# Thresholded attention and SwiGLU on one core: alternating two column tiles of TensorE, and a GpSimd comparison with one operation instead of two

## The chip, the cores and the metric

The kernel runs on one core of a Trainium2 chip. The metric is the device time of one execution in microseconds (us). Lower is better. The program is one launch; matmuls run on TensorE (PE), whose weight loads are shown apart (PEld); VectorE (DVE), ScalarE (ACT) and GpSimd (POOL) do the rest, and SyncE (SP) issues most DMAs.

## The reference

Eight batches, eight heads, 576 rows of queries, keys and values with 64 elements each; then a feed-forward layer over the 4608 rows of 512.

```python
scores = (1 / sqrt(64)) * q @ k.T                      # per batch and head, 576 x 576
thresh = max(scores, axis=-1) - tau                    # tau = 0.02
scores = where(scores >= thresh, scores, -1e9)
attn   = exp(scores - max(scores))
attn   = attn / (sum(attn) + 1e-9)
x      = attn @ v                                      # heads side by side: 4608 x 512
xn     = x / sqrt(mean(x * x) + 1e-6) * rms_g
out    = (silu(xn @ w_gate) * (xn @ w_val)) @ w_out    # 512 -> 1536 -> 512, float32
```

## The kernel before

**Chunks and steps.** The 576 rows of a batch are 4 chunks of 128 rows ("m", ordinary) and 64 last rows. The last rows of two batches together make one "virtual" chunk ("v"): partitions 0 to 63 belong to the first batch, 64 to 127 to the second. There are 32 ordinary and 4 virtual chunks. A step is one chunk with one of 4 pairs of heads, so there are 144 steps; 16 of them are virtual.

**One step.** `emit_s` (line 569) makes the scores of two heads in two PSUM tiles `s_ps`. `emit_softmax` (from line 586) goes on: VectorE reads the scores, negates and scales them into `ssb` and gives each row's minimum `mx` (line 592); GpSimd adds tau to it, `nth` (line 599). Then a head goes one of two ways. In way "p" ScalarE alone drives the elements past the threshold down (line 610) and takes the exponential (lines 614 and 617). In way "g" ScalarE takes the exponential into `esb` (line 629), while GpSimd compares the scores with the threshold, which gives a mask of ones and zeros in `wsb` (line 643), and then multiplies mask by exponential (line 648). From step 16 on the second head of every other step goes way "g", 64 masks in all; the rest goes way "p". The weights `wsb` are turned by a DMA transpose on SP's queue (line 677; in early steps by TensorE, line 662) into `wt`.

**Weights times values.** `emit_av` runs for two steps at a time, so there are 72 blocks, 8 of them virtual. For each step and head, five matmuls accumulate over the 576 keys: four with 65 columns (64 values and a column of ones that gives the sum; line 700) for each head, and one with 130 columns for the last 64 keys of both heads (line 696). In an ordinary block a step has 9 matmuls with weights of 128 columns. In a virtual block the two batches have different values, so the weights are taken 64 columns at a time: rows 0 to 63 of the result with the values of the one batch, rows 64 to 127 with those of the other. These are two column tiles of TensorE, each with 9 matmuls a step, 36 a block.

**Feed-forward.** Groups of 2 or 4 chunks go through `emit_ffn`: gate (line 795), values (line 800), gating on ScalarE and VectorE (lines 809, 812, 817), output (line 865, in the last group line 840).

**Order.** Nothing is ordered by dependence alone. Every operation is entered with an engine, a cost in ns from the table `COST`, a priority and its dependences. `order_ops` (line 44) then plays the whole program through with these costs and gives each engine a fixed order, and hands out the four PSUM buffers `ring` and the places in queues. So a changed cost moves operations on every engine. The cost of a virtual block is twice `av_virt`, that of a mask `mask_g`, 1740 ns. On the chip the engines wait for each other by semaphores, in that order.

Of the kernel before, what the change touches and what calls it, by code (L numbers as in the profile page):

```python
# [11 lines left out]
ALU = mybir.AluOpType  # L12
# [1 line left out]
SEM = 160.0  # L14
SLACK = 0.0
COST = dict(
    s_main=932.0, s_virt=900.0, tr_qk=530.0, tr4=230.0, tr_full=440.0, av_main=310.0, av_virt=480.0, ffn4=216.0, warm=3500.0,
    ttr=690.0, evac_qk=600.0, evac_half=380.0, evac_kt=350.0, prelu=700.0, exp2=1250.0, exp1=690.0, exp0=690.0,
    mask_d=750.0, mask_g=1740.0, take_g=1300.0, trw=510.0, evac_w=450.0, evac_wp=900.0, rz=180.0, xmul=420.0, sq=800.0, xn=720.0,
    pool_tiny=270.0, pool_mean=800.0, pool_dma=850.0, cast_v=650.0, cast_vt=420.0, cast_w=720.0,  # L20
# [107 lines left out]
def kernel(  # L128
# [13 lines left out]
    B, H, S, D = q.shape  # L142
# [40 lines left out]
    ssb = [sb(f"ssb{i}", [128, 2, S]) for i in range(NSS)]  # L183
    NES = 3
    mx = [sb(f"mx{i}", [128, 2]) for i in range(6)]
    nth = [sb(f"nth{i}", [128, 2]) for i in range(6)]
    esb = [sb(f"esb{i}", [128, S], FP16) for i in range(NES)]
    NW = 3
# [39 lines left out]
    for i in range(B // 2):  # L228
        chunks += [("m", 2 * i, c) for c in range(4)]
        at = V_AFTER[i]  # L230
# [355 lines left out]
    def emit_softmax(s, so):  # L586

        a = s % NSS
        m = s % 6
        for h in range(2):  # L590
            def ttr(o, h=h):
                nc.vector.tensor_tensor_reduce(  # L592
                    out=ssb[a][:, h], in0=s_ps[h][:, ROW_AT:ROW_AT + S], in1=zrow, scale=-1.0 / 8.0, scalar=3.0e38,
                    op0=ALU.add, op1=ALU.min, accum_out=mx[m][:, h:h + 1])

            ttr_of[s, h] = add("DVE", COST["ttr"], s - 1, [so, o_c] + exp_of.get(s - NSS, []), ttr)

        def nthr(o):
            nc.gpsimd.tensor_scalar(out=nth[m], in0=mx[m], scalar1=tau, scalar2=None, op0=ALU.add)  # L599

        tn = add("POOL", COST["pool_tiny"], s - 4, [ttr_of[s, 0], ttr_of[s, 1]], nthr)
        wfree = [w_read.get(s - NW)]
        done = []
        ways = WAYS[s % len(WAYS)] if s >= FIRST else "pp"
        pls = []
        for h in range(2):
            way = ways[h]
            if way == "p":
                def prelu(o, h=h):
                    nc.scalar.activation(out=ssb[a][:, h], in_=ssb[a][:, h], func=PRELU, scale=-1.0,  # L610
                                         bias=nth[m][:, h:h + 1], **PRELU_KW)

                def ex(o, h=h):
                    nc.scalar.activation(out=wsb[s % NW][:, h], in_=ssb[a][:, h], func=AF.Exp)  # L614

                def ex2(o):
                    nc.scalar.activation(out=wsb[s % NW], in_=ssb[a], func=AF.Exp)  # L617

                pls.append(add("ACT", COST["prelu"], s + 0.5, [tn], prelu))
                if ways != "pp":  # L620
                    done.append(add("ACT", COST["exp0"], s + 0.5, pls + wfree, ex))
                elif h:
                    done.append(add("ACT", COST["exp2"], s + 0.5, pls + wfree, ex2))
            else:
                es = pre.get("n", 0) % NES
                pre["n"] = pre.get("n", 0) + 1

                def ex(o, h=h, es=es):
                    nc.scalar.activation(out=esb[es], in_=ssb[a][:, h], func=AF.Exp, scale=-1.0,  # L629
                                         bias=nth[m][:, h:h + 1])  # L630

                e = add("ACT", COST["exp1"], s + 0.4, [tn, pre.get(("es", es))], ex)
                if way == "d":
                    def mask(o, h=h, es=es):
                        nc.vector.scalar_tensor_tensor(
                            out=wsb[s % NW][:, h], in0=ssb[a][:, h], scalar=nth[m][:, h:h + 1], in1=esb[es],
                            op0=ALU.is_le, op1=ALU.mult)

                    st = add("DVE", COST["mask_d"], s + 0.4, [e] + wfree, mask)
                    done.append(st)  # L640
                else:
                    def mask(o, h=h):
                        nc.gpsimd.tensor_scalar(  # L643
                            out=wsb[s % NW][:, h], in0=ssb[a][:, h], scalar1=nth[m][:, h:h + 1], scalar2=1.0,
                            op0=ALU.is_le, op1=ALU.mult)

                    def take(o, h=h, es=es):
                        nc.gpsimd.tensor_tensor(out=wsb[s % NW][:, h], in0=wsb[s % NW][:, h], in1=esb[es],  # L648
                                                op=ALU.mult)

                    mk = add("POOL", COST["mask_g"], s + 0.4, [tn] + wfree, mask)
                    st = add("POOL", COST["take_g"], s + 0.4, [e, mk], take)
                    done.append(mk)
                pre["es", es] = st
                done.append(st)
        exp_of[s] = done

        if s < N_PE or s < N_ALT and s % 2:
            def tr(o):
                for j in range(9):  # L660
                    r, c = divmod(j, 5)
                    nc.tensor.transpose(ring[o.slot[r]].bitcast(FP16)[:, 128 * c:128 * c + 128],  # L662
                                        wsb[s % NW].rearrange("p h s -> p (h s)")[:, 128 * j:128 * j + 128], id16)

            t = add("PE", COST["trw"], s + 2.4, done + av_of.get(s - NWT, []), tr, ring="R", nring=2)
            w_read[s] = t
            w_ready[s] = []
            for r, (lo, hi) in enumerate(((0, 5), (5, 9))):
                def ev(o, r=r, lo=lo, hi=hi):
                    eng = nc.gpsimd if W_EVAC[r] == "POOL" else nc.vector  # L670
                    eng.tensor_copy(out=wt[s % NWT][:, lo:hi], in_=ring[t.slot[r]].bitcast(FP16)[
                        :, 0:128 * (hi - lo)].rearrange("p (c n) -> p c n", n=128))

                w_ready[s].append(add(W_EVAC[r], COST["evac_w" if W_EVAC[r] == "DVE" else "evac_wp"], s + 2.4, [t], ev, frees=(t, r)))
        else:
            def tdma(o):
                nc.sync.dma_start_transpose(out=wt[s % NWT], in_=wsb[s % NW].rearrange("p h s -> p (h s)"))

            t = add("SP", COST["sp_tr"], s, done + av_of.get(s - NWT, []), tdma, dma=DMA_NS['wt'])
            w_read[s] = t  # L680
            w_ready[s] = [t]

    def emit_av(s):

        ci, p1 = steps[s]
        kind, b, c = chunks[ci]
        hp = p1 // 2

        def fn(o):
            for i in range(2):  # L690
                w, p = wt[(s - 1 + i) % NWT], p1 - 1 + i
                rows = [(slice(0, 128), b % 2)] if kind == "m" else [(HALF[e], e) for e in range(2)]
                for rs, vi in rows:

                    at = 2 * i * (D + 1)
                    nc.tensor.matmul(ring[o.slot[0]][rs, at:at + 2 * (D + 1)], w[:, 4, rs],  # L696
                                     va[vi][:, p, 8:10].rearrange("p e d -> p (e d)"), start=True, stop=False)
                    for h in range(2):
                        for j in range(4):
                            nc.tensor.matmul(ring[o.slot[0]][rs, at:at + D + 1], w[:, 5 * h + j, rs],  # L700
                                             va[vi][:, p, 2 * j + h], start=False, stop=(h == 1 and j == 3))
                        at += D + 1

        bs = [b] if kind == "m" else [2 * b, 2 * b + 1]
        deps = w_ready[s - 1] + w_ready[s] + [x for bb in bs for i in range(2) for x in v_ready[bb, p1 - i]]
        o = add("PE", 2 * COST["av_main" if kind == "m" else "av_virt"], s + AV_PRIO, deps, fn, ring="R",
                mode=0 if kind == "m" else 3)
        for i in range(2):
            av_of[s - i] = [o]
            for bb in bs:  # L710
                last_av[bb, p1 - i] = last_av.get((bb, p1 - i), []) + [o]

        r = rz[len(half_ev) % 3]

        def half(_):
            o3 = ring[o.slot[0]][:, 0:4 * (D + 1)].rearrange("p (h d) -> p h d", d=D + 1)
            nc.vector.reciprocal(out=r, in_=o3[:, :, D])
            nc.vector.tensor_tensor(  # L718
                out=xsb[ci % 2][:, 256 * hp:256 * hp + 256].rearrange("p (h d) -> p h d", d=D),
                in0=o3[:, :, 0:D], in1=r[:, :, None].to_broadcast([128, 4, D]), op=ALU.mult)  # L720

        half_ev.append(add("DVE", COST["rz"] + COST["xmul"], s + HALF_PRIO, [o] + x_done.get(ci - 2, []), half,
                           frees=(o, 0)))
# [179 lines left out]
    groups, at = [], 0  # L903
# [157 lines left out]
```

## Time and profile before

| | |
|---|---|
| median of 3 runs | 568.4 us (568.31 to 568.87) |
| the profiled execution's own time | 568.4 us |
| its span, first to last instruction | 566.3 us |
| TensorE clock granted | 1.00 |
| busy: PE, PEld | 557.7 us (98%), 318.3 us (56%) |
| busy: DVE, ACT, POOL | 425.1 us (75%), 458.1 us (81%), 354.1 us (63%) |
| masks, line 643 | 64, mean 2219 ns |
| line 700, tiles of 64 columns | 256 matmuls; of 128 columns 1024 |

The times of instructions come from the one profiled execution, so they are set against its 568.4 us; 2.1 us of that lie outside the span. Matmuls are pipelined: an instruction's time in the profile is from its start to its modelled end, and the next one usually starts long before that. What a block of matmuls costs is therefore read from its start to the start of the next. In a row such as `128*64 128x65`, the first pair is the rows and columns of the tile of TensorE, the second the partitions and elements that stream through it.

### The profile page before, as it was taken

How to read it: one execution, taken by the hardware profiler on the slowest of the kernel's cores; microseconds unless marked ns; L12 is line 12 of the kernel's file. 1: busy time of each engine (PE TensorE's matmuls, PEld its weight loads, DVE VectorE, ACT ScalarE, POOL GpSimd, SP SyncE). 2: the span in 40 equal slices, each digit the busy share in tenths (PEclk: the TensorE clock that was granted, in tenths of full speed). 3: DMA queues.
4: the chain of work that ended last, by engine and by line, in shares of the span. 5: the costliest groups of instructions: out<-in, count | busy, mean ns of one | idle time of the engine just before them, and what ended most of it. 6: DMA issues, size and time to landing. Idle time of an engine off the chain costs nothing.

```text
span 566.3 us, 15217 instructions
## 1 busy us (share of the span) xinstructions
PE 557.7 (98%) x5768; PEld 318.3 (56%) x5768; DVE 425.1 (75%) x1091; ACT 458.1 (81%) x741; POOL 354.1 (63%) x462
## 2 busy tenths in 40 slices
PE   8999999999999999999999999999999999999997
PEld 4756666757666555545555455545555444444674
DVE  4989977859968588658985789668966886587354
ACT  5999989897989787888888898798988888785332
POOL 2378956996777467766677676766776765662000
PEclk9999999999999999999999999999999999999999
DMA  9999999779987598879977699888998444552201
GB/s 195 268 298 251 154 205 203 142 155 180 209 181 114 113 174 150 165 161 191 164 153 192 113 165 172 186 178 144 182 183 194 95 94 112 150 86 61 85 38 38
DMA packets 270025, 89.08 MB, mean 157 GB/s; under 512 B 252544, under 2 KB 262272, under 8 KB 269952
## 3 DMA queue, kind: packets, MB, share of 16 engines
q1 hardware_dynamic: 267168, 86.02, 74.3%
q0 software_dynamic: 1600, 1.57, 1.8%
q8 instruction: 45, 0.74, 0.6%
q10 hardware_dynamic: 1184, 0.52, 0.3%
q14 instruction: 28, 0.23, 0.2%
HBM read 37.75 MB, written 9.44 MB: 83 GB/s over the span
## 4 chain that ended last, share of the span: by engine, by line
PE 91%; DVE 3%; ACT 2%; issue 2%; DMA 1%; POOL 1%; SPq 0%; DVEq 0%; ACTq 0%; POOLq 0%
PE s_ps L569 28%; PE ring L795 16%; PE ring L800 16%; PE ring L865 15%; PE ring L700 6%; PE ring L304 2%; PE ring L696 2%; DVE ssb L592 1%; DMA stage<-in_moe_w_gate_dram 1%; PE s_ps L800 1%; PE s_ps L840 1%; PE s_ps L865 1%; PE ring L662 1%; PE ring L365 1%; ACT ssb L610 1%
## 5 line engine op out<-in xcount | busy, mean ns | idle before, releaser
L592 DVE CUSTOM_DVE_ANT_0 ssb<-s_ps,zrow 128x576 f32<-128x576 f32 x288 | 207.0, 752 | 62.5 <-PE s_ps L569 52.1
L610 ACT ACTIVATE ssb<-ssb,nth 128x576 f32<-128x576 f32 x224 | 166.2, 767 | 41.6 <-POOL nth L599 41.2
L569 PE MATMUL s_ps<-qkt 64*64 64x288 f32 (+1 forms) x1792 | 168.9, 417 | 1.6 <-DVE mx L592 1.5
L643 POOL TENSOR_SCALAR wsb<-ssb,nth 128x576 f16<-128x576 f32 x64 | 142.0, 2219 | 8.4 <-DMA wt<-wsb 3.0
L569 PEld LDWEIGHTS s_ps<-qkt 64*64 64x64 f32 (+1 forms) x1792 | 80.0, 140 | 63.8 <-DVE mx L592 16.5
L795 PE MATMUL ring<-xnT,wg 128*128 128x256 f16 (+1 forms) x564 | 114.4, 325 | 0.3 <-DVE xsb L718 0.3
L800 PE MATMUL ring<-xnT,wv 128*128 128x512 f16 (+1 forms) x528 | 110.4, 332 | 0.0
L812 DVE SCALAR_TENSOR_TENSOR sl<-th,ring 128x256 f32<-128x256 f32 (+1 forms) x141 | 77.0, 546 | 37.0 <-ACT th L809 36.3
L599 POOL TENSOR_SCALAR nth<-mx 128x2 f32<-128x2 f32 x144 | 31.9, 221 | 107.6 <-DVE mx L592 86.8
L617 ACT ACTIVATE wsb<-ssb 128x1152 f16<-128x1152 f32 x80 | 93.0, 1162 | 3.2 <-DMA wt<-wsb 1.1
L865 PE MATMUL ring<-wo,hf 128*128 128x512 f16 x384 | 90.0, 380 | 0.0
L648 POOL TENSOR_TENSOR wsb<-wsb,esb 128x576 f16<-128x576 f16 x64 | 81.8, 1278 | 9.7 <-ACT esb L629 5.2
L809 ACT ACTIVATE th<-ring 128x256 f32<-128x256 f32 (+1 forms) x141 | 67.2, 478 | 24.8 <-PE ring L795 20.1
L817 DVE TENSOR_TENSOR hf<-ring,sl 128x512 f16<-128x512 f32 (+1 forms) x132 | 74.9, 567 | 9.3 <-PE ring L800 0.5
L800 PEld LDWEIGHTS <-wv 128*128 128x128 f16 x576 | 52.2, 98 | 44.5 <-issue 14.0
L795 PEld LDWEIGHTS <-wg 128*128 128x128 f16 x576 | 51.9, 98 | 42.3 <-issue 12.3
L865 PEld LDWEIGHTS <-hf 128*128 128x128 f16 x408 | 37.3, 98 | 47.0 <-issue 7.0
L629 ACT ACTIVATE esb<-ssb,nth 128x576 f16<-128x576 f32 x64 | 49.2, 768 | 6.0 <-POOL nth L599 5.7
L700 PE MATMUL ring<-va,wt 128*128 128x65 f16 (+1 forms) x1264 | 52.8, 193 | 0.0
L700 PEld LDWEIGHTS <-wt 128*128 128x128 f16 (+1 forms) x1280 | 48.7, 100 | 4.3 <-issue 1.2
L614 ACT ACTIVATE wsb<-ssb 128x576 f16<-128x576 f32 x64 | 43.6, 681 | 1.6
L696 PE MATMUL ring<-va,wt 128*128 128x130 f16 (+1 forms) x158 | 35.1, 227 | 1.1 <-ACT qTv L473 1.1
(68 smaller groups left out, 446.2 us busy)
## 6 DMA issues: line engine op xcount, KB each, us to landing
vst<-in_v_dram SPq DMA_DIRECT2D x32, 256.0 KB, 3.5
qkn<-in_k_dram SPq DMA_DIRECT2D x31, 256.0 KB, 4.2
out_dram<-osb SPq DMA_DIRECT2D x31, 256.0 KB, 2.7
qkn<-in_q_dram SPq DMA_DIRECT2D x28, 256.0 KB, 4.1
stage<-in_moe_w_gate_dram SPq DMA_DIRECT2D x6, 512.0 KB, 5.9
stage<-in_moe_w_val_dram SPq DMA_DIRECT2D x6, 512.0 KB, 6.0
wt<-wsb SPq DMA_TRANSPOSE x128, 3.1
wo<-in_moe_w_out_dram POOLq DMA_DIRECT2D x4, 384.0 KB, 6.7
```

The source lines that it names most:

```text
L569: nc.tensor.matmul(s_ps[h][rows, ROW_AT + n * part:ROW_AT + n * part + n], lhs(hs), kT[i][p][h][hs, n * part:n * part + n], start=True, st ...
L592: nc.vector.tensor_tensor_reduce(out=ssb[a][:, h], in0=s_ps[h][:, ROW_AT:ROW_AT + S], in1=zrow, scale=-1.0 / 8.0, scalar=3.0e38, op0=ALU.a ...
L610: nc.scalar.activation(out=ssb[a][:, h], in_=ssb[a][:, h], func=PRELU, scale=-1.0, bias=nth[m][:, h:h + 1], **PRELU_KW)
L617: nc.scalar.activation(out=wsb[s % NW], in_=ssb[a], func=AF.Exp)
L643: nc.gpsimd.tensor_scalar(out=wsb[s % NW][:, h], in0=ssb[a][:, h], scalar1=nth[m][:, h:h + 1], scalar2=1.0, op0=ALU.is_le, op1=ALU.mult)
L648: nc.gpsimd.tensor_tensor(out=wsb[s % NW][:, h], in0=wsb[s % NW][:, h], in1=esb[es], op=ALU.mult)
L700: nc.tensor.matmul(ring[o.slot[0]][rs, at:at + D + 1], w[:, 5 * h + j, rs], va[vi][:, p, 2 * j + h], start=False, stop=(h == 1 and j == 3))
L795: nc.tensor.matmul(ring[o.slot[0]][:, 0:n], wg[d][:, fs], xnT[slot][:, d, 0:n], start=(d == 0), stop=(d == 3))
L800: nc.tensor.matmul(ring[o.slot[0]][:, 0:n], wv[d][:, fs], xnT[slot][:, d, 0:n], start=(d == 0), stop=(d == 3))
L812: nc.vector.scalar_tensor_tensor(out=sl[i][:, 0:n], in0=th[i][:, 0:n], scalar=1.0, in1=ring[g.slot[0]][:, 0:n], op0=ALU.add, op1=ALU.mult)
L817: nc.vector.tensor_tensor(out=hf[hi][:, 0:n], in0=ring[vv.slot[0]][:, 0:n], in1=sl[i][:, 0:n], op=ALU.mult)
L865: nc.tensor.matmul(ring[(first or o).slot[0]], hf[hs[fc][0]][:, 128 * j:128 * (j + 1)], wo[:, fc], start=(fc == 0), stop=(fc == NFC - 1))
```

## The change

Two edits, and one entry of the planner's table that goes with the first.

In a virtual block the loop over the two column tiles is moved inside: the two matmuls with 130 columns come first, one for each tile, and then for each head and each quarter of the keys a matmul for the first tile and one for the second. The matmuls are the same, 36 a block, and each tile's own order is kept. In an ordinary block there is one tile, and its order is unchanged. The table's `av_virt` goes from 480 to 320 ns, by which the planner makes another order for all engines from the first virtual block on.

GpSimd's comparison of scores with the threshold loses its second operation, a multiplication by 1.0. The result is the same mask. Its entry in the table, 1740 ns, stays.

```diff
-    ... av_main=310.0, av_virt=480.0, ffn4=216.0, ...
+    ... av_main=310.0, av_virt=320.0, ffn4=216.0, ...

                     def mask(o, h=h):
                         nc.gpsimd.tensor_scalar(
-                            out=wsb[s % NW][:, h], in0=ssb[a][:, h], scalar1=nth[m][:, h:h + 1], scalar2=1.0,
-                            op0=ALU.is_le, op1=ALU.mult)
+                            out=wsb[s % NW][:, h], in0=ssb[a][:, h], scalar1=nth[m][:, h:h + 1], scalar2=None,
+                            op0=ALU.is_le)

                 rows = [(slice(0, 128), b % 2)] if kind == "m" else [(HALF[e], e) for e in range(2)]
+                at = 2 * i * (D + 1)
                 for rs, vi in rows:
-
-                    at = 2 * i * (D + 1)
                     nc.tensor.matmul(ring[o.slot[0]][rs, at:at + 2 * (D + 1)], w[:, 4, rs],
                                      va[vi][:, p, 8:10].rearrange("p e d -> p (e d)"), start=True, stop=False)
-                    for h in range(2):
-                        for j in range(4):
+                for h in range(2):
+                    for j in range(4):
+                        for rs, vi in rows:
                             nc.tensor.matmul(ring[o.slot[0]][rs, at:at + D + 1], w[:, 5 * h + j, rs],
                                              va[vi][:, p, 2 * j + h], start=False, stop=(h == 1 and j == 3))
-                        at += D + 1
+                    at += D + 1
```

More of the change, by code (lines that the diff above doesn't have):

```diff
@@ L16 @@
 COST = dict(
-    s_main=932.0, s_virt=900.0, tr_qk=530.0, tr4=230.0, tr_full=440.0, av_main=310.0, av_virt=480.0, ffn4=216.0, warm=3500.0,
+    s_main=932.0, s_virt=900.0, tr_qk=530.0, tr4=230.0, tr_full=440.0, av_main=310.0, av_virt=320.0, ffn4=216.0, warm=3500.0,
     ttr=690.0, evac_qk=600.0, evac_half=380.0, evac_kt=350.0, prelu=700.0, exp2=1250.0, exp1=690.0, exp0=690.0,
```

## The prediction

> **What bounds the kernel now.** I read the page's busy table and chain first, then the stretches by time, then the blocks that the change touches, one by one.
>
> ```profile
> span 566.3 us, 15217 instructions
> PE 557.7 (98%) x5768; PEld 318.3 (56%) x5768; DVE 425.1 (75%) x1091; ACT 458.1 (81%) x741; POOL 354.1 (63%) x462
> PE 91%; DVE 3%; ACT 2%; issue 2%; DMA 1%; POOL 1%; SPq 0%; DVEq 0%; ACTq 0%; POOLq 0%
> ```
>
> TensorE is busy for 98% and is 91% of the chain that ended last. Its time is the kernel's time, and other engines count only where they make it wait. The stretches say where that is (columns: length; busy time and count of PE, PEld, DVE, ACT, POOL; clock; DMA).
>
> ```profile
> 150.00:200.00 50.00, 48.94 (x543) 31.05 (x543) 36.18 (x101) 42.92 (x73) 33.52 (x40) 1.00 0.77 147
> 200.00:300.00 100.00, 100.00 (x994) 52.95 (x992) 79.94 (x191) 84.51 (x132) 68.34 (x86) 1.00 0.85 166
> ```
>
> From 200 us on TensorE never pauses. Busy time hides short pauses, since the modelled end of a matmul runs on after it, so I also compared every block of matmuls, start to next start, with the fastest of its kind: 10.2 us are lost before 60 us, 7.9 between 60 and 200, 3.7 after that. GpSimd masks exist only from 60.0 to 507.6 us (line 643).
>
> **The weights times values of the virtual chunks.** There are 4 such chunks, of 4 head pairs; a block does two pairs, so there are 8 blocks of 36 matmuls. The chain shows one, and what follows it:
>
> ```profile
> 99.11 0.17 PE ring L696
> ...
> 99.90 0.27 PE ring L700 x10
> 100.17 0.38 PE s_ps L569
> ```
>
> From 99.11 to 100.17 the chain is in this block alone: 1.06 us. Start to next start the 8 blocks take 1.063 to 1.069 us, 8.5 us together. How much of that is one tile waiting for the other? The timeline of TensorE shows the four turns of this block, then one of its weight loads (PEld), and last a block of an ordinary chunk (128 columns, half the matmuls):
>
> ```profile
> 99.04 0.24 PE L696 MATMUL ring<-va,wt 128*64 128x130 f16 x1
> 99.12 0.32 PE L700 MATMUL ring<-va,wt 128*64 128x65 f16 x5
> 99.25 0.24 PE L696 MATMUL ring<-va,wt 128*64 128x130 f16 x1
> 99.47 0.24 PE L696 MATMUL ring<-va,wt 128*64 128x130 f16 x1
> 99.68 0.24 PE L696 MATMUL ring<-va,wt 128*64 128x130 f16 x1
> ...
> 99.25 0.11 PEld L696 LDWEIGHTS <-wt 128*64 128x64 f16 x1
> ...
> 95.33 0.23 PE L696 MATMUL ring<-va,wt 128*128 128x130 f16 x1
> 95.64 0.22 PE L696 MATMUL ring<-va,wt 128*128 128x130 f16 x1
> 96.03 0.45 PE L569 MATMUL s_ps<-qkt 64*64 64x288 f32 x1
> ```
>
> In the ordinary block nine matmuls take 0.31 us (95.33 to 95.64). In the virtual block a new turn of nine, of the same 650 moving columns, starts every 0.21 us. So a column tile already starts while the other still has three or so matmuls left: the two tiles do run side by side, but for only a third of the time, as far as the queue looks ahead. The last turn, with nothing behind it, takes 0.42 us to the next operation (99.68 to 100.10), of which some 0.1 us is the change of tile shape and stays.
>
> Matmul by matmul the partner is always next in the queue, and each tile has its 18 matmuls to itself. A tile then needs what an ordinary block needs, 0.70 us (95.33 to 96.03), plus about 0.03 for a first load that is not hidden: 0.73. Saving 1.066 - 0.73 = 0.33 us a block, **2.6 us** for eight. Bounds: at best 0.70 a block, 2.9 us saved; at worst the tiles take strict turns and lose the overlap that they have: four times 0.31 and 0.1 for the change of shape, 1.34 us a block, 2.2 us lost. I take 2.6, since the loads are seen overlapping: the load of line 696 for the second tile starts at 99.25, inside the first tile's row of matmuls (99.12 to 99.44), and those keep their pace. The score blocks also alternate over four 64x64 tiles and take 1.13 us for 16 matmuls, ones that stream over the same rows among them.
>
> A rule speaks against this. The Trainium skill, "TensorE: Matmul & The Clock Gate", Part 3 (The mechanism), says that weight loads overlap running matmuls only where the row group differs; both tiles here use all 128 rows. By that rule the tiles would take strict turns, and this term would be the loss of 2.2 us. The row at 99.25 is against it, so the measurement decides.
>
> **GpSimd's comparison with one operation.** The mask loses its second operation, a multiplication by 1.0. The rows of GpSimd that bear on it:
>
> ```profile
> L643 POOL TENSOR_SCALAR wsb<-ssb,nth 128x576 f16<-128x576 f32 x64 | 142.0, 2219 | 8.4 <-DMA wt<-wsb 3.0
> L487 POOL TENSOR_SCALAR va<-vst 128x512 f16<-128x512 f32 x32 | 20.0, 625 | 12.6 <-DMA vst<-in_v_dram 11.0 <-DMA vtl<-in_v_dram 0.5
> L487 POOL TENSOR_SCALAR va<-vtl 64x256 f16<-64x256 f32 x16 | 6.5, 404 | 1.1 <-DMA vtl<-in_v_dram 0.5
> ```
>
> Two multiplications cost (625 - 404) / 256 = 0.86 ns an element over some 183 ns fixed; compare and multiply cost (2219 - 183) / 576 = 3.5. Dropping one multiplication at half of 0.86 saves 0.25 us; at half of 3.5 it saves 1.0. The planner's table holds 1740 ns for this mask, and its other GpSimd costs stand 16 to 27 ns above what they measure (cast_w 720 to 693, take_g 1300 to 1278, cast_v 650 to 625), so 1740 reads like a one-operation mask of about 1.72 us, 0.5 less. I take that. No one-operation form of this size is in the trace (the only one, line 599, has 2 elements and 221 ns), so it can also be slower: bounds 1.2 to 3.0 us, the upper end being the same step the other way by 0.8.
>
> 64 masks by 0.5 is 32 us of GpSimd, but GpSimd is 1% of the chain. It counts where the threshold nth (line 599) is queued behind a mask or its product on GpSimd, and ScalarE, and then TensorE, wait for that nth. GpSimd's timeline shows it at one of TensorE's pauses:
>
> ```profile
> 169.97 1.28 POOL L648 TENSOR_TENSOR wsb<-wsb,esb 128x576 f16<-128x576 f16 x1
> 171.33 0.22 POOL L599 TENSOR_SCALAR nth<-mx 128x2 f32<-128x2 f32 x1
> ```
>
> The chain has the scores' minimum ready at 170.08, but nth runs only at 171.33, once the product of line 648 is through; at 173.8 TensorE loses 1.2 us. Between 60 and 200 us nine pauses are over 0.3 us. If all nine shrank by 0.5 that would be 4.5 us; if none, nothing. In some of them nth stands behind other work, or a DVE or DMA comes last, so I take about a quarter to a third, **1.3 us**.
>
> **The order.** av_virt goes from 480 to 320 in the planner, used twice for a block, so every engine's order after the first virtual block (about 99 us) is new. The work is not: the same matmuls, with 97 score blocks on four tiles instead of 96 (1.13 against 1.07 us each: 0.06 us). With each kind at its duration, TensorE's listed work falls by 2.6 us, all of it the virtual blocks. Score blocks move ahead of feed-forward work by up to 6 us in the middle. On SP a load of k now waits behind one more transpose of weights, on GpSimd two casts of v stand ahead of a mask instead of after it. Their cover is the TensorE work that lies between a score block and the weights times values that need it: 10.9 to 18.3 us in the old order from step 16 on, 11.2 to 18.3 in the new; the path of mask, product and transpose (2.2, 1.3 and 3.1 us) is 6.6 us. I take 0, with 2 us to either side.
>
> **The sum.** The profiled execution took 568.4 us for a span of 566.3, 2.1 outside it, and equals the median. 568.4 - 2.6 - 1.3 = **564.5 us**.
>
> **Rivals.** (1) The one-operation mask is slower. At 3.0 us, 0.8 more, the nine pauses would each grow by up to 0.8: 7.2 - 2.6 = 4.6, so 573.0 us. It decides from 2.6 / 9 = 0.3 us on, a mask of 2.5 us. For it: every other sizeable GpSimd cast carries a neutral second operation. Against it: fewer operations, and the planner's 1740. (2) The alternation does not do what it says: the tiles take strict turns, 568.4 + 2.2 - 1.3 = 569.3. Against it the overlap at 99.25. (3) The new order brings new pauses that eat the gain, as the old order has of 0.3 to 1.2 us each: five of 0.7 give 568.0. For it: 7.9 us of such pauses between 60 and 200 us, where TensorE is at its tightest against DVE, ACT and GpSimd (ACT busy 42.9 of 50 us in the first row of stretches); against it: almost none after 200 us.
>
> **How the numbers follow.** The forecast has 0.68, rival 1 0.14, rival 2 0.06, rival 3 0.12. The forecast's bounds: 2.9 + 4.5 off gives 561.0; upward, 2.6 off and 2 us of pauses given back gives 567.8. The range goes on to 569.5, taking in rivals 2 and 3 and the mild part of 1. A difference of 0.2% (1.1 us) is about what a measurement of this kernel tells from none. Faster (under 567.3): the forecast and its milder neighbours of rival 3, 0.71. Same: the rest of rival 3 and most of rival 2, 0.14. Slower: nearly all of rival 1 and the rest of 2, 0.15.
>
> **What would show it.** Right: virtual blocks of 0.70 to 0.76 us, first matmuls of the two tiles a few ns apart; the mask's row near 1720 ns; TensorE still 98% busy; blocks between 60 and 200 us losing less than 7.9 us. Wrong: blocks at 1.06 us or more (rival 2), a mask over 2.5 us with more wait of ACT for nth (rival 1), or as much PE work gone but longer pauses after 100 us (rival 3).

## The result: 0.9% faster, and where it came from

| | before | after |
|---|---|---|
| median of 4 runs | 568.5 us | 562.97 us |
| runs | 568.31 to 568.87 | 562.58, 562.82, 563.12, 564.9 |
| ratio, with its 95% interval | | 0.9909 (0.9885 to 0.9932) |
| profiled execution, its span | 568.4, 566.3 us | 564.9, 562.9 us |

The profiled execution is the slowest of the four. One execution of the mask alone (below) took 689.08 us at a granted clock of 0.754, where every other execution here had 0.975 or more; the ratio leaves it out. The page of after:

```profile
span 562.9 us, 15231 instructions
PE 552.9 (98%) x5776; PEld 315.4 (56%) x5776; DVE 425.6 (76%) x1091; ACT 458.9 (82%) x741; POOL 322.5 (57%) x462
PE 92%; DMA 3%; DVE 2%; ACT 1%; issue 1%; POOL 0%; DVEq 0%; POOLq 0%; ACTq 0%
```

TensorE still sets the end. GpSimd's busy time fell by 31.6 us and its 1% of the chain is gone. DMA's share went from 1% to 3%; two pieces of the chain of waits show part of that:

```profile
84.53 4.75 DMA wt<-wsb
...
89.32 0.23 PE ring L695
```

TensorE waits here for one transpose of weights. Before, none stood on the chain at this place. SP's queue had been held up earlier by a transpose that took 5.33 us to issue (3.28 before). The profile of the alternation alone (below) has a like event (4.13 us, and 1.8 us of waiting for weights at 87 us), although its first virtual block starts only at 100.7 us and it has the order and the mask of before: nothing that it changes had run by then. The profiles of the mask alone and of both edits in the old order lose no such time there. So I count it to the execution, not to the change.

The first virtual block of after, in the timeline of TensorE and then its first weight loads:

```profile
101.14 0.25 PE L695 MATMUL ring<-va,wt 128*64 128x130 f16 x2
101.22 0.42 PE L700 MATMUL ring<-va,wt 128*64 128x65 f16 x16
101.48 0.22 PE L695 MATMUL ring<-va,wt 128*64 128x130 f16 x2
101.54 0.42 PE L700 MATMUL ring<-va,wt 128*64 128x65 f16 x16
101.89 0.47 PE L569 MATMUL s_ps<-qkt 64*64 64x288 f32 x4
...
101.14 0.11 PEld L695 LDWEIGHTS <-wt 128*64 128x64 f16 x2 [0.21 <-issue]
101.17 0.11 PEld L700 LDWEIGHTS <-wt 128*64 128x64 f16 x2
```

The four turns (99.04, 99.25, 99.47, 99.68 before) have become two, and the loads of the two tiles go in pairs (x2 in one row). From 101.14 to 101.89 is 0.74 us; all eight blocks take 0.741 to 0.744, where 1.063 to 1.069 was. The mask's group:

```profile
L643 POOL TENSOR_SCALAR wsb<-ssb,nth 128x576 f16<-128x576 f32 x64 | 110.5, 1726 | 12.8 <-DMA wt<-wsb 6.9
```

1726 ns, down from 2219. So both parts did to their own instructions what was forecast (0.73 us and 1.72 us). What each is worth to the whole had to be measured.

### The profile page after: what moved, and what is told of

Read it like the earlier page. It is cut to its first block, busy times and chain, and to the rows that moved or that the text cites. A ratio compares the mean times of both kernels' runs of the same rounds, so it can differ in the third digit from the quotient of the medians.

```text
span 562.9 us, 15231 instructions
## 1 busy us (share of the span) xinstructions
PE 552.9 (98%) x5776; PEld 315.4 (56%) x5776; DVE 425.6 (76%) x1091; ACT 458.9 (82%) x741; POOL 322.5 (57%) x462
## 3 DMA queue, kind: packets, MB, share of 16 engines
q0 software_dynamic: 1600, 1.57, 1.9%
## 4 chain that ended last, share of the span: by engine, by line
PE 92%; DMA 3%; DVE 2%; ACT 1%; issue 1%; POOL 0%; DVEq 0%; POOLq 0%; ACTq 0%
PE s_ps L569 29%; PE ring L800 16%; PE ring L795 16%; PE ring L865 14%; PE ring L700 6%; DMA wt<-wsb 2%; PE ring L304 2%; PE ring L695 2%; DVE ssb L592 1%; PE ring L662 1%; DMA qkn<-in_q_dram 1%; PE s_ps L840 1%; PE s_ps L865 1%; PE ring L365 1%; PE s_ps L795 1%
## 5 line engine op out<-in xcount | busy, mean ns | idle before, releaser
L610 ACT ACTIVATE ssb<-ssb,nth 128x576 f32<-128x576 f32 x224 | 166.4, 767 | 31.6 <-POOL nth L599 31.2
L643 POOL TENSOR_SCALAR wsb<-ssb,nth 128x576 f16<-128x576 f32 x64 | 110.5, 1726 | 12.8 <-DMA wt<-wsb 6.9
L569 PEld LDWEIGHTS s_ps<-qkt 64*64 64x64 f32 (+1 forms) x1800 | 79.4, 140 | 61.1 <-DVE mx L592 16.2
L800 PE MATMUL ring<-xnT,wv 128*128 128x512 f16 (+1 forms) x548 | 112.9, 329 | 0.0
L795 PE MATMUL ring<-xnT,wg 128*128 128x512 f16 (+1 forms) x544 | 111.9, 328 | 0.3 <-DVE xsb L718 0.3
L812 DVE SCALAR_TENSOR_TENSOR sl<-th,ring 128x512 f32<-128x512 f32 (+1 forms) x136 | 75.1, 553 | 21.9 <-ACT th L809 20.7
L809 ACT ACTIVATE th<-ring 128x512 f32<-128x512 f32 (+1 forms) x136 | 65.7, 485 | 26.3 <-PE ring L795 23.3
L817 DVE TENSOR_TENSOR hf<-ring,sl 128x512 f16<-128x512 f32 (+1 forms) x137 | 76.8, 561 | 9.8
L700 PE MATMUL ring<-va,wt 128*128 128x65 f16 (+1 forms) x1264 | 50.4, 193 | 0.0
L700 PEld LDWEIGHTS <-wt 128*128 128x128 f16 (+1 forms) x1280 | 46.1, 100 | 4.3 <-issue 0.7
L695 PE MATMUL ring<-va,wt 128*128 128x130 f16 (+1 forms) x158 | 31.8, 225 | 2.4 <-DMA wt<-wsb 1.6
```

Of the source, the lines that this page charges most:

```text
L569: nc.tensor.matmul(s_ps[h][rows, ROW_AT + n * part:ROW_AT + n * part + n], lhs(hs), kT[i][p][h][hs, n * part:n * part + n], start=True, st ...
L643: nc.gpsimd.tensor_scalar(out=wsb[s % NW][:, h], in0=ssb[a][:, h], scalar1=nth[m][:, h:h + 1], scalar2=None, op0=ALU.is_le)
L795: nc.tensor.matmul(ring[o.slot[0]][:, 0:n], wg[d][:, fs], xnT[slot][:, d, 0:n], start=(d == 0), stop=(d == 3))
L800: nc.tensor.matmul(ring[o.slot[0]][:, 0:n], wv[d][:, fs], xnT[slot][:, d, 0:n], start=(d == 0), stop=(d == 3))
L812: nc.vector.scalar_tensor_tensor(out=sl[i][:, 0:n], in0=th[i][:, 0:n], scalar=1.0, in1=ring[g.slot[0]][:, 0:n], op0=ALU.add, op1=ALU.mult)
L817: nc.vector.tensor_tensor(out=hf[hi][:, 0:n], in0=ring[vv.slot[0]][:, 0:n], in1=sl[i][:, 0:n], op=ALU.mult)
```

## Experiments

Each ratio is against runs of the kernel before on the same chip, timed beside it, with its 95% interval; a time difference worked out from it is (ratio - 1) x 568.5.

**The parts, one by one.** The alternation alone:

```diff
 after, with
-    av_virt=320.0
+    av_virt=480.0
 ...
-    ... scalar2=None, op0=ALU.is_le)
+    ... scalar2=1.0, op0=ALU.is_le, op1=ALU.mult)
```

> The alternation alone: two-operation mask, av_virt still 480, so every engine's order is that of before. My theory (each block falls from 1.066 to about 0.74 us, all of it on TensorE's path): virtual blocks of 0.74 us and 2.6 us less in all, 565.9 us. Rival, that the blocks' gain is given back as longer waits for VectorE, since the scores come sooner after them: blocks of 0.74 us, but less than 1.3 us gained, 567.2 us or more.

567.65 us, 0.9978 (0.9969 to 0.9987): 1.25 us less. The blocks are 0.740 to 0.744 us, so 2.6 us of TensorE work is gone, and half of that gain was given back as waits. (This profile is of the slowest of eleven executions, 568.61 us, and holds the event at 87 us besides; the views below are from 200 us on.) The waits of TensorE's weight loads between 200 and 520 us (us in all, times, longest), in before:

```profile
PEld s_ps L569 <- DVE mx L592: 7.8, 20, 0.4
```

and in this kernel:

```profile
PEld s_ps L569 <- DVE mx L592: 10.1, 26, 0.4
```

The next scores come sooner and find VectorE not yet done with the last ones: score blocks that run longer than the fastest of their kind lose 3.1 us after 200 us, 2.3 in before. That is the rival's case: blocks of 0.74 us, and less than 1.3 us gained.

The mask alone:

```diff
 before, with
-    ... scalar2=1.0, op0=ALU.is_le, op1=ALU.mult)
+    ... scalar2=None, op0=ALU.is_le)
```

> The one-operation mask alone: blocks tile by tile, order of before. My theory (a shorter mask gives nth earlier at some of TensorE's pauses between 60 and 200 us): mask 1.73 us, 1.3 us less, 567.2 us, bounds 0 to 4.5; pauses of TensorE between 60 and 200 us fall from 7.9 to about 6.6 us. Rival, that GpSimd is off the path and the whole remaining gain is the new order's: within 0.5 us of before.

564.29 us, 0.9925 (0.9911 to 0.9938): **4.3 us less**, near the upper bound of 4.5 and over three times the 1.3 taken. Blocks of matmuls against the fastest of their kind in these runs, virtual blocks apart, lose 4.9 us between 60 and 200 us (7.1 before) and 1.7 after 200 (3.7 before). So nearly half of the gain came from the stretch where the forecast saw nothing to gain. The pause that the forecast shows, at 173.8 us, shrank from 1.23 to 0.75 us, by as much as the mask.

The planner's entry alone:

```diff
 before, with
-    av_virt=480.0
+    av_virt=320.0
```

> The planner's entry alone, av_virt 320: the order of the changed kernel, with blocks tile by tile and the two-operation mask. The recorded forecast took 0 for the order, with 2 us to either side: 568.5 us. If instead the new order carries what the change gained beyond the 2.6 us of the blocks, this run is near 565.6 us. If the order only pays when the blocks are as short as it assumes, it is slower than before, by up to 1 us.

569.41 us, 1.0011 (1.0002 to 1.0020): 0.6 us more. The new order costs a little, with the long mask at least.

Both edits in the old order:

```diff
 after, with
-    av_virt=320.0
+    av_virt=480.0
```

> Both edits with av_virt 480, so the order of before. If the parts add up and the order is worth nothing: 568.5 - 2.6 - 1.3 = 564.6 us by the forecast's terms, and the same as the changed kernel (563.0) within 0.5 us if mask and blocks together carry all of it. If the order carries the rest: 2.6 us less than before and no more, 565.9 us.

561.88 us, 0.9891 (0.9875 to 0.9907): 6.2 us less, the fastest kernel here by its ratio. Set against the mask alone, the alternation is worth 0.9925 - 0.9891 = 0.0034, 1.9 us. That is more than its 1.25 with the long mask, but the intervals don't tell the two apart.

**A third order.** `av_virt=371.0`, half of the 742 ns that a block takes, in place of 480 in the kernel just above.

> Alternation and one-operation mask with av_virt 371, so that the planner holds exactly what a block measures (2 x 371 = 742 ns). A third order for the same work. If the order's cost in the change (about 1 us between 480 and 320) comes from entries that differ from the measured times: at least as fast as with 480, 561.9 us or less. If orders differ by chance: anywhere from 560.5 to 564.5 us.

562.37 us, 0.9894 (0.9876 to 0.9911), not told apart from 480. The changed kernel's 0.9909 lies within this interval and just above the one with 480, and its own interval (0.9885 to 0.9932) holds both ratios. So with both edits the order's part (0.6 to 1.1 us by the medians) is not separated from nothing.

**Why the short mask pays: occupancy or the weights' own path?** The mask is both a stretch in which GpSimd can't compute the next nth, and the first link to the weights. An idle instruction behind the product, into a new tile `dump` that nobody reads, restores the one and not the other:

```diff
 mask alone, with
     nc.gpsimd.tensor_tensor(out=wsb[s % NW][:, h], in0=wsb[s % NW][:, h], in1=esb[es], op=ALU.mult)
+    nc.gpsimd.tensor_scalar(out=dump, in0=zrow[:, 0:360], scalar1=1.0, scalar2=1.0, op0=ALU.mult, op1=ALU.mult)
```

> The one-operation mask alone (564.3 us, 4.3 less than before), plus an idle two-operation GpSimd instruction of about 0.5 us (360 elements into a tile that nobody reads) behind each of the 64 products. GpSimd is then as long occupied as in before, so nth waits as long there, but the weights come as early as with the short mask. Theory A (occupancy: nth queued behind the mask's pair): the gain goes, 567.5 to 569 us, ScalarE's wait for nth between 200 and 520 us back from 22 to about 33 us. Theory B (the weights' own path): the gain stays, 563.8 to 565 us.

567.52 us, 0.9988 (0.9978 to 0.9997): of 4.3 us 0.7 are left. The padding measured 495 ns, what the mask had lost. The waits between 200 and 520 us, first of before:

```profile
ACT ssb L610 <- POOL nth L599: 33.0, 30, 2.4
DVE sl L812 <- ACT th L809: 18.0, 26, 1.7
```

Of the mask alone:

```profile
ACT ssb L610 <- POOL nth L599: 22.3, 27, 2.0
...
DVE sl L812 <- ACT th L809: 12.9, 25, 1.3
```

And of the mask with the padding, whose lines stand two or four further down:

```profile
ACT ssb L612 <- POOL nth L601: 36.1, 36, 2.3
DVE sl L816 <- ACT th L813: 19.4, 25, 1.6
```

This is the path: nth is late, ScalarE's queue stands, its tanh for the feed-forward (`th`) is late, VectorE's queue stands before `sl`, and behind that are the reads of the scores, for which TensorE waits. Both waits come and go with GpSimd's occupancy, and the trace links them: of VectorE's waits for `th`, 13.6 of 18.0 us in before follow directly on a wait of ScalarE for nth, 6.4 of 12.9 with the mask alone, 16.2 of 19.4 with the padding. At TensorE's end, a score block of before that takes 1.57 us, not the 1.13 of an undisturbed one, and the wait inside it:

```profile
444.93 1.57 PE s_ps L569 x16
...
445.30 0.69 PEld L569 LDWEIGHTS s_ps<-qkt,qTv 64*64 64x64 f32 x14 [0.26 <-DVE mx L592]
```

After 200 us such score blocks lose 2.3 us in before, 0.2 with the mask alone and 2.3 with the padding: all that the mask regains in this stretch. The pause at 173.8 us is back too, 1.21 us. About 0.7 us (0.2 to 1.3 by the interval) doesn't come back; more than that the weights' own path doesn't carry.

**The other direction: the mask issued twice.**

```diff
 mask alone, with
+    ... (the same nc.gpsimd.tensor_scalar a second time)
```

> Order and blocks of before, and the one-operation mask issued twice in a row into the same tile (same result): 2 x 1.73 = 3.45 us for each of 64 masks, 1.23 more than before's 2.22. If time follows the mask as between 1.73 and 2.22 us (4.3 us for 0.49, 8.7 us per us of mask): 10.7 us more, 579 us. If GpSimd then falls behind altogether, well over that, 590 us. If the short mask's gain was a chance of one set of alignments: under 3 us more.

599.61 us, 1.0535 (1.0515 to 1.0554): 30 us more. From 1.73 to 2.22 us a mask costs 8.7 us of time per us, from 2.22 to 3.45 some 25. GpSimd's busy time is only 83 of 100 us (columns: PE, PEld, DVE, ACT, POOL):

```profile
300.00:400.00 100.00, 95.35 (x966) 50.09 (x965) 68.32 (x170) 79.54 (x125) 82.96 (x96) 1.00 0.78 155
```

and TensorE already idles for nearly 5 of them. So here GpSimd sets the time while it is far from full. The weights' own path is 1.2 us longer too, and TensorE waits four times for a transpose of weights (2.0 us in all, none in before), so the steeper slope is not nth's alone.

**Taking nth off GpSimd.** If nth in GpSimd's queue is the cause, VectorE could compute it:

```diff
 before, with
-    nc.gpsimd.tensor_scalar(out=nth[m], in0=mx[m], scalar1=tau, scalar2=None, op0=ALU.add)
+    nc.vector.tensor_scalar(out=nth[m], in0=mx[m], scalar1=tau, scalar2=None, op0=ALU.add)
```

> Before with one thing changed: nth (line 599, threshold of two heads) is computed by VectorE, at the same place of the order, not by GpSimd; the two-operation mask stays at 2.22 us, blocks tile by tile. Theory A (the mask costs time because nth is queued behind it on GpSimd, and ScalarE, VectorE and then TensorE wait for nth): most of what the short mask brought comes here as well, 3 to 5 us less, 564 to 566 us, and ScalarE's wait for nth (33.0 us between 200 and 520 us) falls under 20. Theory B (TensorE waits for the weights themselves, mask, product and transpose): no more than 0.5 us less, 568 us or above, less the 144 x 0.06 us that VectorE gets more of.

572.45 us, 1.007 (1.0053 to 1.0088), 4 us more. ScalarE's wait for nth did fall, to 23.2 us (not under 20), but this is no clean test, because a new cost came with it. An instruction of 2 elements takes 325 ns on average, 47 us of VectorE in all. Its group:

```profile
L599 DVE TENSOR_SCALAR nth<-mx 128x2 f32<-128x2 f32 x144 | 46.8, 325 | 1.2
```

One of them in VectorE's timeline, and GpSimd's at that moment:

```profile
144.54 1.09 DVE L599 TENSOR_SCALAR nth<-mx 128x2 f32<-128x2 f32 x1
...
144.33 1.28 POOL L648 TENSOR_TENSOR wsb<-wsb,esb 128x576 f16<-128x576 f16 x1 [0.41 <-ACT esb L629]
```

The product on GpSimd ends at 144.33 + 1.28 = 145.61, nth at 144.54 + 1.09 = 145.63. Of the 144 nth, 41 take over 300 ns (median of all 164), and 38 of these end 20 to 30 ns after the end of a GpSimd instruction that was running when they began. The Trainium skill, "Advanced Engine Details and Errata", VectorE Performance Modes (Mode Summary), notes that VectorE's second SBUF port is shared with GpSimd and that two-port instructions and GpSimd's block each other. The rows agree with that; which mode VectorE chose, no run here shows. The long ones make up 23 of the 47 us by what they take over 164 ns. That VectorE's new load is all of the 4 us is likely, but not shown.

With both edits and nth on VectorE (the fastest kernel above, the same line changed):

> Alternation and one-operation mask with av_virt 480 (the fastest so far, 561.9 us), and nth on VectorE. Theory A: no nth waits for GpSimd any more, so the pauses that are left after 60 us (about 7 us) shrink again and the alternation keeps its 2.6 us: 558 to 561 us. Theory B, or VectorE being the tighter engine: 561.5 us or more.

569.3 us, 1.0016 (0.9999 to 1.0032). Worse by 7.1 us, by the ratios, than with nth on GpSimd. The profile has the same rows: 29 nth over 300 ns, 26 of them ending 22 to 28 ns after a GpSimd instruction that ran when they began. Whether nth on GpSimd is the cause, these two runs can't say; that rests on the padding.

**Is one operation always cheaper?** The kernel's other GpSimd conversions all carry a second multiplication, by 1.0:

```diff
 both edits in the old order, with, on lines 487, 737 and 937,
-    ... scalar2=1.0, op0=ALU.mult, op1=ALU.mult)
+    ... scalar2=None, op0=ALU.mult)
```

> Alternation and one-operation mask with av_virt 480, and GpSimd's other conversions (values, weights, normalised x: lines 487, 737, 937) with one multiplication instead of two. If every operation costs its 0.85 ns an element, as the mask's second did ((2219 - 1727) / 576): 128x512 conversions fall from 625 and 694 ns by 0.43 us each, and the time by up to 1 us from 561.9. If a single multiplication is bound by reading and writing: the rows and the time unchanged. If the one-operation form is a slower one for multiplication: rows over 700 ns, and the time above 562.5 us.

605.61 us, 1.0651 (1.0635 to 1.0667). Not all of these 37 us need be GpSimd's own time: the granted TensorE clock was 0.91 up to 60 us and 0.94 from there to 200, 1.00 in before. The conversions more than double, where the mask had become shorter:

```profile
L737 POOL TENSOR_SCALAR xn<-xsb,ir 128x512 f16<-128x512 f32 x36 | 56.7, 1575 | 3.7
L487 POOL TENSOR_SCALAR va<-vst 128x512 f16<-128x512 f32 x32 | 48.0, 1502 | 12.3 <-DMA vst<-in_v_dram 9.0 <-PE ring L304 1.7 <-DMA vtl<-in_v_dram 0.3
...
L487 POOL TENSOR_SCALAR va<-vtl 64x256 f16<-64x256 f32 x16 | 13.6, 850 | 0.6
```

One multiplication costs (1502 - 850) / 256 = 2.55 ns an element, two cost 0.86 (before). One comparison costs about (1726 - 190) / 576 = 2.67, taking as fixed the 190 ns of the one-element instruction of line 732; comparison and multiplication 3.5. So one operation alone, of either kind, is near 2.6 ns, a second one after a comparison adds 0.86, and the pair of multiplications is a special, fast case. Why, no run here shows.

**How fine must the turns be?** The changed kernel with turns of four matmuls of one tile, and with turns of two, one run of each:

```diff
 after, with (turns of four)
-                for h in range(2):
-                    for j in range(4):
-                        for rs, vi in rows:
+                for h in range(2):
+                    for rs, vi in rows:
+                        for j in range(4):
```

> The changed kernel, but with turns of four matmuls (one head of one tile, then the same head of the other). If the queue looks about three matmuls past a waiting one, as the blocks of before suggest (the second tile started with three left of nine), a turn of four hides nearly all: blocks of 0.75 to 0.85 us. If matmuls of different tiles run side by side only when they are neighbours: near 1.0 us.

> The changed kernel, but with turns of two matmuls of each tile. Looking about three ahead: the full effect, 0.74 us a block. Neighbours only: 0.85 to 0.95 us.

Turns of four: blocks of 0.767 to 0.771 us (563.31 us). Turns of two: 0.741 to 0.744 (562.24 us), as with single matmuls. So it isn't neighbours that pair, and the look-ahead that the turns of nine showed is real: about three matmuls of one tile are passed over for one of the other. A rival, that matmuls are handed out at one about every 24 ns (nine in the 0.21 us of a turn before), does not fit: the alternating block starts its 36 within 0.62 us, one every 18 ns. A block's timeline with turns of four still has the two tiles' 130-column matmuls in one row (x2), and 0.77 us to the next operation:

```profile
98.73 0.25 PE L695 MATMUL ring<-va,wt 128*64 128x130 f16 x2
98.81 0.45 PE L700 MATMUL ring<-va,wt 128*64 128x65 f16 x16
...
99.50 0.47 PE L569 MATMUL s_ps<-qkt 64*64 64x288 f32 x4
```

## Why the prediction came out, and which of its terms did not

The time, 562.97 us against 564.5, lies in the range, and the sign is right. But that is luck in part: the sum is near by terms that were off in opposite directions.

- **The blocks: right in size, wrong in worth.** 0.742 us measured, 0.73 forecast; 2.59 us of TensorE work removed, 2.6 forecast (2.7 unrounded). The rule on weight loads and row groups did not hold for column tiles: the loads at 101.14 run in pairs over the same 128 rows, and the strict turns that it would have meant did not come. The step that failed is "568.4 - 2.6": work taken off an engine on the path is worth all of itself only if nothing else is next. By the runs it was worth 1.25 us with the long mask and 1.9 with the short one. Of the rest, some 0.8 us shows in the profile of the alternation alone as longer score blocks, where TensorE waits for VectorE; where the remainder went is open.
- **The mask: duration right, worth mis-sized.** 1726 ns measured, 1720 read out of the planner's table (whose entry for nth, left out there, stands 49 ns above its row, not 16 to 27). The path through nth was right. The 1.3 us should have been 4.3. Two steps failed. "From 200 us on TensorE never pauses" was read from busy time, though the same paragraph counts 3.7 us of pauses there; the mask got back 2.0 of them, some 0.9 in pauses of under 0.3 us. And between 60 and 200 us a quarter to a third of the 4.5 us was taken, where the nine pauses shrank by 2.0 us together and short ones by 0.2.
- **The order.** 0 was taken. The runs show 0.6 us of loss with the old parts, not separated from nothing with the new ones. The 2 us to either side held.
- **The sum.** The parts alone give 1.25 + 4.26 - 0.63 = 4.9 us; the change measured 5.2 by its ratio, 3.9 was forecast.
- **Rival 1** (a slower one-operation mask) did not come, but was not idle: the one-operation form is much slower for multiplications. Its price was far too low. Interpolated between 2.22 and 3.45 us, a mask of 3.0 would have cost about 19 us (an estimate from the mask issued twice), not 7.2. The point from which it decides, put at 0.3 us more, would be near 0.1 by the same slope (2.6 / 25).
- **Rival 3** came in small: the order's 0.6 us.

## What to carry to other kernels

Where one engine is busy for 98%, price a change elsewhere by who queues behind it: 0.5 us more in each of 64 instructions, on an engine that is 1% of the chain, cost 4.3 us here because a tiny threshold instruction shared its queue. Work removed from the bound engine is worth its length only as far as the next wait allows: 1.25 of 2.6 us here. The two edits together gained 6.2 us against 5.5 for their sum, which the intervals don't tell apart. Alternate column tiles in turns of one or two matmuls, and measure a GpSimd instruction in exactly the form that will be used.

## What the runs showed of the hardware that I had not expected

- On GpSimd, float32 to float16, one multiplication by a scalar takes 1502 ns for 128x512 and two take 625; a comparison alone takes 1726 for 128x576, and with a multiplication 2219. The Trainium skill, "GPSIMD Engine Reference", section 3.1, has bodies of up to two operations bound by the ports at 1.03 cycles an element; by an estimate from that and its 1.2 GHz, 0.86 ns. The pair of multiplications agrees (0.86), the single operations (2.55 to 2.67) do not.
- A VectorE instruction of 2 elements, 164 ns in the median, took up to 1.9 us while GpSimd worked; 38 of the 41 long ones (up to 1.2 us) stood until a running GpSimd instruction was over.
- Two column tiles over the same 128 rows load weights and stream at the same time at nearly the pace of one: 18 matmuls of each in 0.742 us, where 18 of one 128-column tile take 0.70. In turns of nine, four and two, TensorE starts the second tile's work up to about three matmuls ahead (blocks of 1.066, 0.769 and 0.742 us).
